# A third block-product group in the second layer of a retention and two-FFN kernel

## The chip, the cores and the metric

The kernel runs on one core of a Trainium2 chip. The metric is the device time of one execution in microseconds, as the median of several runs. A profile of one execution goes with it: it gives a span from the first to the last instruction, and every time below that has a position ("at 505 us") counts from the start of that span. PE is TensorE (PEld its weight loads), DVE is VectorE, ACT is ScalarE, SP is the engine that issues the DMAs.

## What is computed

```python
x = retention(q, k, v, lam)            # 2 batches x 768 tokens, 8 heads of 64 -> 1536 x 512
h = x @ w_in1;  g = h * tanh(softplus(h));            x = g @ w_out1    # 512 -> 2048 -> 512
h = x @ w_in2;  g = where(h > 0, h, exp(min(h, 0)) - 1); out = g @ w_out2   # 512 -> 2048 -> 512
```

All in float32. Each operand of a matrix product is held as two parts, high and low, whose sum it is, and a product is made of three matmuls (high x high, high x low, low x high).

## The kernel before

The 1536 tokens are three tiles of 512 (t = 0, 1, 2), the 2048 inner columns of a layer four groups of 512 (g = 0 to 3). One layer, group and token tile make a *step*, numbered s = 12 l + 3 g + t, so the second layer has steps 12 to 23: 18, 19, 20 are its third group and 21, 22, 23 its fourth. An **in** unit (s, i) makes 128 inner columns by 12 matmuls of 512 columns (`mm_in`, L487) and applies the activation; in the second layer that is `elu`: two ScalarE steps (L514, L515), one VectorE step (L516), and then a split into the two parts (`split_g`, `in_two`: ScalarE L160, VectorE L161). An **out** unit (s, d) multiplies the four inner tiles of a step by the second weights, 12 matmuls (`mm_out`, L652), and `flush` adds the result to the accumulator `acc` on VectorE (L680); in the last group it also sends it to memory. The very last out unit is done in two pieces, with 24 matmuls.

**Block products.** In groups 1 to 3 of the first layer and in the last group of the second, token tiles 1 and 2 are multiplied together by seven block products in place of eight (`block_product`, L608; z = 0, 1 are the two halves of the group's columns). A half takes 42 matmuls where the plain way takes 48. It needs, beforehand, four sums of weight blocks (`later_sums(g, z)`: ten VectorE additions of 256 columns, L151, and a split) and, once a layer, sums of token blocks (`token_sums`: additions of 1024 columns, and splits). Of the seven products of a half, 1, 6, 7 and 4 are added up in one PSUM bank, with a copy by ScalarE (`keep`, L617) after 1, 6 and 7; `done` adds these copies to the other banks on VectorE (L621) and the activation follows.

**Weights.** Each pair of weight tiles is loaded into one of two `raw` buffers and turned into two parts by `w_steps`: eight VectorE instructions of 1024 columns (L119 to L146) and a ScalarE copy (L143). They work in a tile with the tag `m`, of which there are two; `later_sums` and `token_sums` take their scratch tiles from the same two. The list `PAIRS` says after which unit a pair's instructions stand in the program. A pair writes into a buffer that an earlier group's weights must have left.

**Order.** The list `seq` is the program's order of units. Up to the last step it alternates: in s, out s-1. Then come out 21 and the products of group 3, then out 22 and out 23. The framework's planner fixes each engine's queue when the kernel is built: by program order, but an instruction whose inputs and buffers its plan holds ready may pass one whose are not. At run time each queue stands in that order.

`all_out` does the four out units of a step at once: four PSUM tiles, with the inner tile as the outer loop, so that the second inner tile is needed only after 12 matmuls and the third after 24. Before the change it serves step 0 alone.

Of the kernel before, what the change touches and what calls it, by code (L numbers as in the profile page):

```python
# [8 lines left out]
F32 = mybir.dt.float32  # L9
# [9 lines left out]
def kernel(  # L19
# [130 lines left out]
    def plus(out, a, b, op=ALU.add):  # L150
        nc.vector.tensor_tensor(  # L151
            out=out.bitcast(F32), in0=a.bitcast(F32), in1=b.bitcast(F32), op=op
        )

    def minus(out, a, b):
        plus(out, a, b, ALU.subtract)
# [363 lines left out]

    mx = {}

    def later_sums(g, z):

        x = cv.tile([P, 2 * DM], I32, tag="m", name="x").bitcast(F32)
        s1, s2, s3, s4 = (x[:, y * 2 * P:(y + 1) * 2 * P] for y in range(4))
        h, l = (
            [wts[1, 0, g * G + 2 * z + j][:, n, k * 2 * P:(k + 1) * 2 * P]
             for j in range(2) for k in range(2)] for n in range(2)
        )  # L530
        plus(s1, h[2], h[3])
        minus(s3, h[0], h[2])
        plus(s1, s1, l[2])
        plus(s3, s3, l[0])
        plus(s1, s1, l[3])
        minus(s3, s3, l[2])
        minus(s2, s1, h[0])
        minus(s2, s2, l[0])
        minus(s4, h[1], s2)
        plus(s4, s4, l[1])  # L540
        t = wp.tile([P, 2, 2, DM], F32R, tag=f"w{z}", name="sl", bufs=2)
        in_two([t[:, n].rearrange("p j c -> p (j c)") for n in range(2)], x)
        sums[1, g, z] = t.rearrange("p n j (y c) -> p n (j y) c", y=2)

    def token_sums(l):

        xs = [(xh[t][:, h * 2:h * 2 + 2], xl[t][:, h * 2:h * 2 + 2]) for t in (1, 2) for h in range(2)]
        b11, b21, b12, b22 = xs  # L550
        if l == 0:
            t2, t3, t4 = (
                late["t"].tile([P, 2, 2, TB], F32R, tag=f"t{x}", name=f"t{x}") for x in (2, 3, 4)
            )
            x, y = acc[2][:, 0:2], acc[2][:, 2:4]
        else:
            t2, t3 = (
                cv.tile([P, 2, KD, P, 2], I32, tag="raw", name="tl").bitcast(F32R).rearrange(
                    "p n a b c -> p n (a b c)").rearrange("p n (k f) -> p n k f", k=2)
                for _ in range(2)  # L560
            )
            t4 = late["w"].tile([P, 2, 2, TB], F32R, tag="t4", name="t4", bufs=1)
            x, y = (
                cv.tile([P, 2 * DM], I32, tag="m", name="x").bitcast(F32).rearrange(
                    "p (k f) -> p k f", k=2) for _ in range(2)
            )
        t2, t3, t4 = ((t[:, 0], t[:, 1]) for t in (t2, t3, t4))
        minus(x, b22[0], b12[0])
        minus(y, b22[1], b12[1])
        plus(x, x, y)  # L570
        in_two(t3, x)
        minus(x, b12[0], b11[0])
        minus(y, b12[1], b11[1])
        plus(x, x, y)
        minus(y, b22[0], x)
        plus(y, y, b22[1])
        in_two(b12, x)
        minus(x, b21[0], y)
        plus(x, x, b21[1])
        in_two(t2, y)  # L580
        in_two(t4, x)
        mx["b"] = {
            1: b11, 2: b21, 3: b22, 4: t4, 5: b12, 6: t2, 7: t3,
        }

    def block_product(l, g, z, x):


        w = [wts[l, 0, g * G + 2 * z + j] for j in range(2)]
        sm = sums[l, g, z]  # L590
        def of(j, h):
            return [w[j][:, n, h * 2 * P:(h + 1) * 2 * P] for n in range(2)]
        a = {1: of(0, 0), 2: of(0, 1), 4: of(1, 1)}.get(x)
        if a is None:
            y = {5: 0, 6: 1, 7: 2, 3: 3}[x]
            a = [sm[:, n, y] for n in range(2)]
        b = mx["b"][x]
        bank = {1: 0, 6: 0, 7: 0, 4: 0, 2: 1, 5: 2, 3: 2}[x]
        fresh = x in (1, 2, 5)
        if fresh:  # L600
            pool, tag = ((late["psY"], "y"), (late["psH"], "h"))[z]
            mx[z, bank] = pool.tile([P, TB], F32, tag=tag, name="mb" + tag)
        ps = mx[z, bank]
        for kk in range(2):
            ha, la = (t[:, kk * P:(kk + 1) * P] for t in a)
            hb, lb = (t[:, kk] for t in b)
            for n, (lt, rt) in enumerate(((ha, hb), (ha, lb), (la, hb))):
                nc.tensor.matmul(  # L608
                    ps, lhsT=lt, rhs=rt, start=fresh and kk == 0 and n == 0,
                    stop=kk == 1 and n == 2, skip_group_check=True,  # L610
                )
        s1, s2 = (l * NG + g) * NTB + 1, (l * NG + g) * NTB + 2
        i1, i2 = 2 * z, 2 * z + 1

        def keep(y):
            mx[z, "c", y] = tp.tile([P, TB], F32, tag="e", name="c", bufs=ES)
            nc.scalar.activation(out=mx[z, "c", y], in_=ps, func=AF.Copy)  # L617

        def done(y, s, i):
            c = mx[z, "c", y]  # L620
            nc.vector.tensor_tensor(out=c, in0=c, in1=ps, op=ALU.add)  # L621
            if l == 0:
                nc.scalar.activation(out=c, in_=c, func=AF.Mish)
                mid[s, i] = c
            else:
                elu(s, i, c)
            split_g(s, i)

        if x in (1, 6, 7):
            keep({1: 1, 6: 2, 7: 3}[x])  # L630
        if x == 2:
            done(1, s1, i1)
        elif x == 3:
            done(2, s2, i1)
        elif x == 4:
            (mish, elu)[l](s1, i2, ps)
            split_g(s1, i2)
        if x == 7:
            ps = mx[z, 2]
            done(3, s2, i2)  # L640
# [17 lines left out]
    def all_out(s):  # L658

        l, g, t = steps[s]  # L660
        ys = [late["psY"].tile([P, TB], F32, tag="y", name="y") for _ in range(KD)]
        for i in range(G):
            w, gg = wts[l, 1, g * G + i], gt[s, i]
            for d, y in enumerate(ys):
                a = [w[:, n, d * P:(d + 1) * P] for n in range(2)]
                for n, (lt, rt) in enumerate(((a[0], gg[:, 0]), (a[0], gg[:, 1]), (a[1], gg[:, 0]))):
                    nc.tensor.matmul(  # L667
                        y, lhsT=lt, rhs=rt,
                        start=(i == 0 and n == 0), stop=(i == G - 1 and n == 2),
                    )  # L670
        for d, y in enumerate(ys):
            flush(s, d, slice(0, TB), y)
# [42 lines left out]
        if g < NG - 1:  # L715
            add_units("out", s + 2)
    LAST = NS - NTB
    for s in range(NG * NTB, LAST + 1):
        add_units("in", s)
        add_units("out", s - 1)  # L720
    seq.extend(("out", LAST, d) for d in range(2))
    for z in range(2):
        seq.extend(("mix", (1, NG - 1, z), x) for x in range(3))
        seq.append(("out", LAST, 2 + z))
        seq.append(("mix", (1, NG - 1, z), 3))
    add_units("out", LAST + 1)
    add_units("out", LAST + 2)

    def unit(u):
        kind, s, x = seq[u]  # L730
        if kind == "mix":
            for y in MIX[x]:
                block_product(*s, y)
        elif kind == "in":
            (mish, elu)[steps[s][0]](s, x, mm_in(s, x))
            if late:
                split_g(s, x)
        else:

            if s == 0:  # L740
                if x == 0:
                    all_out(s)
                return
            ends = (0, 3 * TB // 4, TB) if u == len(seq) - 1 else (0, TB)
            for c0, c1 in zip(ends, ends[1:]):
                cols = slice(c0, c1)
                flush(s, x, cols, mm_out(s, x, cols))
# [4 lines left out]
    BESIDE = 4  # L752
    PAIRS = {
        0: (None, None, 0, 3), 1: (12, 12, 23, 25), 2: (37, 41, 47, 49), 3: (61, 65, 71, 73),
        4: (82, 84, 88, 91),
    }
    TOKENS = 11
    at = {}
# [3 lines left out]
            if u is not None:  # L762
                at.setdefault(u, []).append(g * PG + 2 * y)
    LAST_MIX = max(u for u, x in enumerate(seq) if x[0] == "mix" and x[1][0] == 0)
    LATE = seq.index(("out", LAST - 2, 0))
    HALVES = 2
    LOAD = {5: ((0, 0),), 8: ((0, 1),), 9: (1,), 10: (2,), 11: (3,), 12: (4, 5), 13: (6, 7)}
    STEPS = {
# [21 lines left out]
    def weights_at(u):  # L790
        if u == LAST_MIX:
            late["mix"].close()
            late["w"] = ctx.enter_context(tc.tile_pool(name="w2p", reuse_waits="tile", bufs=1))
        for n in at.get(u, ()):
            for last_step[n] in w_steps(n, both=True):
                pass
        if u == TOKENS:
            with tc.issue_after(last_step[PG - 2].ins):
                token_sums(0)
        if u == LATE:  # L800
            token_sums(1)
            for z in range(2):
                later_sums(NG - 1, z)

    def first_units():
        with tc.issue_after(made[-2].ins):
# [45 lines left out]
```

## Time and profile before

| | |
|---|---|
| median of 3 runs (lowest, highest) | 577.12 us (576.69, 578.01) |
| the profiled execution: own time, span | 577.09 us, 574.9 us |
| TensorE busy | 565.7 us, 98% |
| VectorE busy | 483.3 us, 84% |
| ScalarE busy | 253.7 us, 44% |
| granted TensorE clock | 1.0 of full speed |

The span is the stretch from the first to the last instruction; the profiled execution's own time is 2.2 us more. A busy time is a sum over the whole span, in which stages with different limits lie one behind the other. Matmuls overlap in the records: one of 512 columns lasts about 390 ns, but a run of them starts at a shorter pitch, which is what counts.

### The profile page before, as it was taken

Reading aid. Unit: us, or ns where it says so; the run is one execution under the profiler, and the core shown is the slowest. Engines: PE = TensorE matmul, PEld = TensorE weight load, DVE = VectorE, ACT = ScalarE, POOL = GpSimd, SP = SyncE. Lnnn points to the kernel's source line nnn. Section 1 sums busy time; section 2 is a strip of 40 time slices with the busy share of each in tenths; the row PEclk is TensorE's granted clock in tenths of the full one; section 3 lists DMA queues with packets and bytes.
Section 4 is the critical chain, followed back from the end, with each engine's and each line's share of the span. In section 5 each row is a group of like instructions: output and inputs, shape, how many; then the busy total and the mean of one; then the engine's idle time right before and its main releaser. Section 6 shows DMA issues by size and latency. Waiting matters only on the chain.

```text
span 574.9 us, 7879 instructions
## 1 busy us (share of the span) xinstructions
PE 565.7 (98%) x3186; PEld 472.6 (82%) x3186; DVE 483.3 (84%) x670; ACT 253.7 (44%) x401; POOL 18.8 (3%) x28
## 2 busy tenths in 40 slices
PE   8999999999999999999999999999999999999987
PEld 7899888887888888888888888888888888888866
DVE  7779999999999979889989899898998766894452
ACT  3655554453542352422646447535425325333540
POOL 5330000000000000000000000000000000000000
PEclk9999999999999999999999999999999999999999
DMA  9998242121312421032222204404311000001004
GB/s 182 202 206 222 78 143 75 73 75 52 100 68 75 146 75 39 35 125 77 91 75 73 74 0 148 145 2 146 95 52 74 0 1 0 1 1 38 36 0 147
DMA packets 61043, 46.64 MB, mean 81 GB/s; under 512 B 38864, under 2 KB 55504, under 8 KB 61008
## 3 DMA queue, kind: packets, MB, share of 16 engines
q1 hardware_dynamic: 60864, 46.14, 26.9%
q8 instruction: 25, 0.41, 0.3%
q14 instruction: 10, 0.08, 0.0%
q10 hardware_dynamic: 144, 0.00, 0.0%
HBM read 43.00 MB, written 3.15 MB: 80 GB/s over the span
## 4 chain that ended last, share of the span: by engine, by line
PE 95%; DMA 2%; SPq 1%; DVE 1%; ACT 0%; issue 0%
PE y L652 43%; PE h L487 30%; PE mby L608 7%; PE mbh L608 7%; PE o L341 3%; PE y L667 2%; PE sc L327 2%; SPq L205 1%; DMA qn<-in_q_dram 1%; DMA vn<-in_v_dram 1%; PE st L373 1%; PE Tp L283 1%; DVE c L621 0%; DVE g L161 0%; ACT g L160 0%
## 5 line engine op out<-in xcount | busy, mean ns | idle before, releaser
L487 PE MATMUL h<-xh,w 128*128 128x512 f32 x512 | 161.9, 390 | 0.0
L652 PE MATMUL y<-w,g 128*128 128x512 f32 (+2 forms) x588 | 135.2, 387 | 2.4 <-ACT g L160 2.0
L652 PEld LDWEIGHTS y<-w,g 128*128 128x128 f32 x588 | 109.3, 188 | 25.6 <-ACT g L160 2.5
L652 PE MATMUL y<-g,w 128*128 128x512 f32 x528 | 124.9, 389 | 0.0
L652 PEld LDWEIGHTS y<-g,w 128*128 128x128 f32 x528 | 99.1, 188 | 20.5
L487 PEld LDWEIGHTS h<-xh,w 128*128 128x128 f32 x512 | 96.1, 188 | 20.1 <-issue 0.2
L487 PE MATMUL h<-xl,w 128*128 128x512 f32 x256 | 99.7, 390 | 0.0
L680 DVE TENSOR_TENSOR acc<-acc,y 128x512 f32<-128x512 f32 (+1 forms) x73 | 48.5, 676 | 23.0 <-PE y L652 22.8
L487 PEld LDWEIGHTS h<-xl,w 128*128 128x128 f32 x256 | 48.1, 188 | 10.0
L514 ACT ACTIVATE e<-h 128x512 f32<-128x512 f32 x40 | 23.7, 596 | 58.1 <-PE h L487 57.1
L146 DVE TENSOR_TENSOR w<-m,w 128x1024 fp32r<-128x1024 f32 (+2 forms) x35 | 39.6, 1130 | 8.2 <-ACT w L143 8.2
L143 ACT ACTIVATE w<-m 128x1024 fp32r<-128x1024 f32 (+2 forms) x35 | 34.4, 982 | 25.7 <-PE y L652 17.4
L129 DVE SCALAR_TENSOR_TENSOR raw<-raw,m 128x1024 int32<-128x1024 int32 (+2 forms) x35 | 39.4, 1130 | 0.2
L136 DVE SCALAR_TENSOR_TENSOR m<-raw,m 128x1024 f32<-128x1024 uint32 (+2 forms) x35 | 39.2, 1130 | 0.3
L139 DVE TENSOR_TENSOR m<-raw,m 128x1024 f32<-128x1024 f32 (+2 forms) x35 | 39.1, 1130 | 0.2
L161 DVE TENSOR_TENSOR g<-e,g 128x512 fp32r<-128x512 f32 x48 | 32.9, 688 | 6.7 <-ACT g L160 6.5
L160 ACT ACTIVATE g<-e 128x512 fp32r<-128x512 f32 x48 | 30.0, 627 | 17.1 <-DVE e L516 17.0
L510 ACT ACTIVATE g<-h 128x512 f32<-128x512 f32 x24 | 14.4, 598 | 45.0 <-PE h L487 44.9
L516 DVE SCALAR_TENSOR_TENSOR e<-e,h 128x512 f32<-128x512 f32 x40 | 27.2, 684 | 7.3 <-ACT e L515 7.3
L515 ACT ACTIVATE e<-e 128x512 f32<-128x512 f32 x48 | 30.0, 629 | 1.0
L119 DVE TENSOR_SCALAR m<-raw 128x1024 int32<-128x1024 int32 (+2 forms) x35 | 22.1, 643 | 5.1 <-DMA raw<-in_moe_w_out_dram 3.5
L678 ACT ACTIVATE acc<-y 128x512 f32<-128x512 f32 x24 | 13.9, 599 | 27.6 <-PE y L652 21.0
(141 smaller groups left out, 671.2 us busy)
## 6 DMA issues: line engine op xcount, KB each, us to landing
raw<-in_moe_w_out_dram SPq DMA_DIRECT2D x32, 512.0 KB, 4.1
raw<-in_moe_w_in_dram SPq DMA_DIRECT2D x31, 512.0 KB, 4.9
vn<-in_v_dram SPq DMA_DIRECT2D x12, 256.0 KB, 5.7
kn<-in_k_dram SPq DMA_DIRECT2D x11, 256.0 KB, 5.2
qn<-in_q_dram SPq DMA_DIRECT2D x11, 256.0 KB, 5.3
out_dram<-acc SPq DMA_DIRECT2D x11, 256.0 KB, 2.0
raw<-in_moe_w_in_dram SPq DMA_DIRECT2D x2, 256.0 KB, 5.6
kn<-in_k_dram SPq DMA_DIRECT2D x2, 128.0 KB, 3.4
```

The source lines that it names most:

```text
L129: yield nc.vector.scalar_tensor_tensor(out=b, in0=b, scalar=-0x40000000, in1=m, op0=ALU.bitwise_and, op1=ALU.bitwise_or)
L136: yield nc.vector.scalar_tensor_tensor(out=mf, in0=lw, scalar=2.0 ** -52, in1=mf, op0=ALU.mult, op1=ALU.mult)
L139: yield nc.vector.tensor_tensor(out=mf, in0=bf, in1=mf, op=ALU.add)
L143: nc.scalar.activation(out=w0, in_=mf, func=AF.Copy)
L146: yield nc.vector.tensor_tensor(out=w1, in0=mf, in1=w0.bitcast(F32), op=ALU.subtract)
L160: nc.scalar.activation(out=t[0], in_=x, func=AF.Copy)
L161: nc.vector.tensor_tensor(out=t[1], in0=x, in1=t[0].bitcast(F32), op=ALU.subtract)
L487: nc.tensor.matmul(h, lhsT=lt, rhs=rt, start=(kk == 0 and n == 0), stop=(kk == KD - 1 and n == 2),)
L515: nc.scalar.activation(out=e, in_=e, func=AF.Exp, scale=-1.0)
L608: nc.tensor.matmul(ps, lhsT=lt, rhs=rt, start=fresh and kk == 0 and n == 0, stop=kk == 1 and n == 2, skip_group_check=True,)
L652: nc.tensor.matmul(y, lhsT=lt, rhs=rt, start=(i == 0 and n == 0), stop=(i == G - 1 and n == 2),)
L680: nc.vector.tensor_tensor(out=dst, in0=dst, in1=y, op=ALU.add)
```

## The change

Group 2 of the second layer (steps 18, 19, 20) is also done by block products for token tiles 1 and 2, and the first token tile's steps of both last groups (18 and 21) are put in front: in 18, out 17, out 18, in 21, and only then the products. Since the two in steps 19 and 20 fall away, the weights of group 3 (`PAIRS[7]`) stand 7 to 21 units earlier in the program than before, its first-side weights being used from the first matmul of in 21. `token_sums(1)` is cut in two: one part behind in 17, which writes the new block over half of `xh[2]`, `xl[2]`, and one behind in 21, which writes over `xh[0]`, `xl[0]`. The four calls of `later_sums` are spread over units 151 to 174, and their results go to `raw` buffers or to weight buffers that are free. In the second layer all PSUM banks of the products come from the pools of the in units, bank 0 (product 1) from the one with a single buffer. Out units of steps 21, 19 and 20 are written out by hand between the products. Step 22, the last but one, goes through `all_out`. The core of the diff:

```diff
-        t = wp.tile([P, 2, 2, DM], F32R, tag=f"w{z}", name="sl", bufs=2)
+        if (g, z) in ((2, 0), (3, 1)):
+            t = raw_place()
+        else:
+            t = wp.tile([P, 2, 2, DM], F32R, tag=f"w{(g, z) == (3, 0):d}", name="sl", bufs=2)
...
-    def token_sums(l):
+    def token_sums(l, part=0):
...
+        if l == 0 or part == 0:
+            minus(x, b12[0], b11[0])
+            minus(y, b12[1], b11[1])
+            plus(x, x, y)
+            minus(y, b22[0], x)
+            plus(y, y, b22[1])
+            in_two(b12, x)
...
+        elif part == 0:
+            t2 = late["w"].tile([P, 2, 2, TB], F32R, tag="t2", name="t2", bufs=1)
+            mx["t2"] = t2[:, 0], t2[:, 1]
+            in_two(mx["t2"], y)
+            return
+        else:
+            t2 = mx["t2"]
+            t3, t4 = ((z[:, 0:2], z[:, 2:4]) for z in (xh[0], xl[0]))
+            minus(x, t2[0], b11[0])
+            minus(y, t2[1], b11[1])
+            plus(x, x, y)
+            in_two(t3, x)
...
+            minus(x, b21[0], t2[0])
+            minus(y, b21[1], t2[1])
+            plus(x, x, y)
+            in_two(t4, x)
...
+            if l == 1:
+                pool, tag = (late["psH"], psH)[x == 1], "h"
...
-    for s in range(NG * NTB, LAST + 1):
+    AGO = LAST - NTB
+    for s in range(NG * NTB, AGO + 1):
         add_units("in", s)
         add_units("out", s - 1)
-    seq.extend(("out", LAST, d) for d in range(2))
-    for z in range(2):
-        seq.extend(("mix", (1, NG - 1, z), x) for x in range(3))
-        seq.append(("out", LAST, 2 + z))
-        seq.append(("mix", (1, NG - 1, z), 3))
+    add_units("out", AGO)
+    add_units("in", LAST)
+    for x in (
+        (LAST, 0), (2, 0, (1, 2)), (2, 0, (6, 5)), (2, 0, (7,)), (LAST, 1), (2, 0, (4, 3)),
+        (LAST, 2), (2, 1, (1, 2)), (2, 1, (6, 5)), (2, 1, (7,)), (LAST, 3), (2, 1, (4, 3)),
+        (3, 0, (2,)), (AGO + 1, 0), (3, 0, (1,)), (AGO + 1, 1), (AGO + 1, 2),
+        (3, 0, (6, 5)), (3, 0, (7,)), (AGO + 1, 3), (3, 0, (4, 3)), (AGO + 2, 0),
+        (3, 1, (1, 2)), (3, 1, (6, 5)), (AGO + 2, 1), (3, 1, (7,)), (AGO + 2, 2),
+        (AGO + 2, 3), (3, 1, (4, 3)),
+    ):
+        seq.append(("out", *x) if len(x) == 2 else ("mix", (1, *x[:2]), x[2]))
     add_units("out", LAST + 1)
     add_units("out", LAST + 2)
...
-            if s == 0:
+            if s in (0, LAST + 1):
                 if x == 0:
                     all_out(s)
                 return
...
-        4: (82, 84, 88, 91),
+        4: (82, 84, 88, 91), 7: (134, 137, 148, 150),
...
-    LATE = seq.index(("out", LAST - 2, 0))
+    LATE = seq.index(("out", AGO - 2, 0))
+    BEHIND = seq.index(("in", LAST, G - 1))
+    SUMS = {
+        151: (2, 0), seq.index(("mix", (1, 2, 0), (4, 3))): (2, 1),
+        seq.index(("mix", (1, 2, 1), (4, 3))): (3, 0),
+        seq.index(("mix", (1, 3, 0), (4, 3))) - 1: (3, 1),
+    }
```

In the new program units 136 to 139 are out 16, 140 to 143 in 18, 144 to 151 out 17 and out 18, 152 to 155 in 21, and 156 is the first of the written-out list.

## Rows read from the trace of the kernel before

**Rows 1.** The page: busy time of the engines; busy tenths in 40 slices.

```profile
PE 565.7 (98%) x3186; PEld 472.6 (82%) x3186; DVE 483.3 (84%) x670; ACT 253.7 (44%) x401; POOL 18.8 (3%) x28
...
PE   8999999999999999999999999999999999999987
...
DVE  7779999999999979889989899898998766894452
```

**Rows 2.** The chain that ended last: start us, us, what.

```profile
505.41 13.60 PE y L652 x60
...
552.05 2.73 PE mbh L608 x12
```

**Rows 3.** TensorE in order of time, last stage: start us, us, instructions, [idle before].

```profile
541.28 2.60 PE L652 MATMUL y<-w,g 128*128 128x512 f32 x9
543.72 1.53 PE L608 MATMUL mbh<-tl,sl 128*128 128x512 f32 x6
545.09 2.88 PE L652 MATMUL y<-w,g 128*128 128x512 f32 x12
547.81 1.52 PE L608 MATMUL mbh<-tl,sl 128*128 128x512 f32 x6
549.17 2.88 PE L652 MATMUL y<-w,g 128*128 128x512 f32 x12
...
556.81 3.02 PE L652 MATMUL y<-w,g 128*128 128x512 f32 x12 [2.04 <-ACT g L160]
560.12 11.86 PE L652 MATMUL y<-w,g 128*128 128x512 f32 x60 [0.30 <-DVE acc L680]
```

**Rows 4.** ScalarE in order of time, second layer.

```profile
449.68 1.06 ACT L143 ACTIVATE w<-m 128x1024 fp32r<-128x1024 f32 x1 [6.87 <-PE y L652]
...
553.45 0.60 ACT L514 ACTIVATE e<-mbh 128x512 f32<-128x512 f32 x1
```

**Rows 5.** VectorE in order of time, second layer.

```profile
407.12 2.36 DVE L136 SCALAR_TENSOR_TENSOR m<-raw,m 128x1024 f32<-128x1024 uint32 x2
...
419.70 1.29 DVE L119 TENSOR_SCALAR m<-raw 128x1024 int32<-128x1024 int32 x2 [0.64 <-DMA raw<-in_moe_w_out_dram]
...
438.64 1.22 DVE L151 TENSOR_TENSOR x<-xh 128x1024 f32<-128x1024 f32 x1
...
452.52 1.22 DVE L151 TENSOR_TENSOR x<-xl 128x1024 f32<-128x1024 f32 x1
...
483.42 1.23 DVE L161 TENSOR_TENSOR xl<-x,xh 128x1024 fp32r<-128x1024 f32 x1 [0.47 <-ACT xh L160]
...
492.45 1.76 DVE L151 TENSOR_TENSOR x<-x,w 128x256 f32<-128x256 f32 x5
...
497.63 1.23 DVE L161 TENSOR_TENSOR sl<-x,sl 128x1024 fp32r<-128x1024 f32 x1 [1.13 <-ACT sl L160]
...
510.03 0.69 DVE L119 TENSOR_SCALAR m<-raw 128x1024 int32<-128x1024 int32 x1
...
556.79 0.69 DVE L161 TENSOR_TENSOR g<-e,g 128x512 fp32r<-128x512 f32 x1 [0.69 <-ACT g L160]
...
558.78 0.69 DVE L161 TENSOR_TENSOR g<-e,g 128x512 fp32r<-128x512 f32 x1 [0.70 <-ACT g L160]
559.39 2.47 DVE L680 TENSOR_TENSOR acc<-acc,y 128x512 f32<-128x512 f32 x4
```

**Rows 6.** Busy time by stretch: PE, PEld, DVE, ACT, POOL, each with its count.

```profile
389.00:419.00 30.00, 30.00 (x134) 24.86 (x133) 27.04 (x36) 15.41 (x25) 0.00 (x0) 1.00 0.40 139
419.00:440.00 21.00, 21.00 (x95) 17.38 (x94) 19.67 (x27) 6.84 (x12) 0.00 (x0) 1.00 0.13 51
440.00:462.00 22.00, 22.00 (x99) 18.23 (x98) 16.13 (x20) 9.10 (x15) 0.00 (x0) 1.00 0.00 0
462.00:472.60 10.60, 10.60 (x48) 8.78 (x47) 6.74 (x10) 2.31 (x4) 0.00 (x0) 1.00 0.01 2
```

**Rows 7.** Groups by shape: busy us, mean ns, idle before it and its enders.

```profile
L621 DVE TENSOR_TENSOR c<-c,mbh 128x512 f32<-128x512 f32 x3 | 2.1, 689 | 3.4 <-ACT c L617 2.7 <-PE mbh L608 0.7
```

More of the change, by code (lines that the diff above doesn't have):

```diff
@@ L521, with raw_place @@
     mx = {}
+    def raw_place():
+        t = cv.tile([P, 2, KD, P, 2], I32, tag="raw", name="tl").bitcast(F32R)
+        return t.rearrange("p n a b c -> p n (a b c)").rearrange("p n (k f) -> p n k f", k=2)
     def later_sums(g, z):
@@ L554, in token_sums @@
             )
+            t2, t3, t4 = ((t[:, 0], t[:, 1]) for t in (t2, t3, t4))
             x, y = acc[2][:, 0:2], acc[2][:, 2:4]
-        else:
[L557 to L562, printed above, removed]
+            minus(x, b22[0], b12[0])
+            minus(y, b22[1], b12[1])
+            plus(x, x, y)
+            in_two(t3, x)
+        else:
             x, y = (
@@ L566, in token_sums @@
             )
[L567 to L581, printed above, removed]
+        if l == 0 or part == 0:
[5 more added lines that the diff above has]
+            in_two(b12, x)
+        if l == 0:
+            minus(x, b21[0], y)
+            plus(x, x, b21[1])
+            in_two(t2, y)
+            in_two(t4, x)
[10 more added lines that the diff above has]
+            plus(x, x, y)
+            in_two(t3, x)
+            x, y = (
+                cv.tile([P, 2 * DM], I32, tag="m", name="x").bitcast(F32).rearrange(
+                    "p (k f) -> p k f", k=2) for _ in range(2)
+            )
+            minus(x, b21[0], t2[0])
+            minus(y, b21[1], t2[1])
+            plus(x, x, y)
+            in_two(t4, x)
         mx["b"] = {
@@ L630, in block_product @@
             keep({1: 1, 6: 2, 7: 3}[x])
-        if x == 2:
+        if x in (1, 2):
+            mx.setdefault((l, g, z), []).append(x)
+        if x in (1, 2) and len(mx[l, g, z]) == 2:
+            ps = mx[z, 1]
             done(1, s1, i1)
@@ L664, in all_out @@
             for d, y in enumerate(ys):
-                a = [w[:, n, d * P:(d + 1) * P] for n in range(2)]
-                for n, (lt, rt) in enumerate(((a[0], gg[:, 0]), (a[0], gg[:, 1]), (a[1], gg[:, 0]))):
+                a, b = (w, gg) if l == 0 else (gg, w)
+                a = [a[:, n, d * P:(d + 1) * P] for n in range(2)]
+                for n, (lt, rt) in enumerate(((a[0], b[:, 0]), (a[0], b[:, 1]), (a[1], b[:, 0]))):
                     nc.tensor.matmul(
@@ L731, in unit @@
         if kind == "mix":
-            for y in MIX[x]:
+            for y in x if s[0] else MIX[x]:
                 block_product(*s, y)
@@ L801, in weights_at @@
             token_sums(1)
-            for z in range(2):
-                later_sums(NG - 1, z)
+        if u == BEHIND:
+            token_sums(1, 1)
+        if u in SUMS:
+            later_sums(*SUMS[u])
     def first_units():
```

## The prediction

> **What bounds the kernel now.** I read the page's busy times and slices first, then the chain of waits, then the order of TensorE over the last 35 us, and only then VectorE's queue and its busy time by stretch. TensorE is busy for 98% of the span, and full in every slice but the first and the last two [rows 1]. The chain that ended last says the same: it runs along TensorE, a run of 60 matmuls in 13.60 us, so 0.2267 us for each [rows 2]. So a matmul taken away is worth its pitch, as long as nothing else comes late. VectorE, at 84%, is the engine that can make it late: nine tenths and more in many slices of the second half, half busy or less in the last four [rows 1].
>
> The last two slices are short of TensorE for another reason [rows 3]. From 541.28 to 560.12 us it starts 9, 6, 12, 6, 12, then the 12 of the chain's last run of products [rows 2], then 12: 69 matmuls, worth 15.64 us, in 18.84 us. So 3.20 us are lost: 0.40 before the products at 543.72; 2.20 before 556.81, where the activation of the last products has not arrived; 0.59 before 560.12, waiting for a flush to free a PSUM tile. The activation's path can be read off: ScalarE starts it at 553.45 [rows 4], VectorE's split ends at 557.48 [rows 5], 4.03 us. The planner had nothing left to put there: of the 48 matmuls of out 22, which stand behind all products in the program, the runs of 9, 12 and 12 at 541.28, 545.09 and 549.17 are already the greater part. Only 12 were kept for the time after the last product.
>
> **The change part by part.**
>
> *Matmuls.* Two halves of a group at 42 in place of 48: 12 fewer, 12 x 0.2267 = 2.72 us [rows 2].
>
> The Trainium skill (TensorE: Matmul & The Clock Gate, "Wait — 56ns, not 53.3ns?") gives 215.7 ns from start to start for 512 columns at full clock. The trace differs, with 226.7 ns at a granted clock of 1.0. By the page the part would be 2.59 us; the measurement decides.
>
> *The end.* In the new order product 4, whose activation was late, is followed by product 3 (6 matmuls) and by all four tiles of step 22 with the inner tile as outer loop, so that its result is wanted after 6 + 24 matmuls, 6.8 us later. The path takes 4.03 us. The first of the four PSUM tiles is finished 9 matmuls (2.04 us) before the last, and a flush takes (2.47 - 0.69) / 3 = 0.59 us in a row of four [rows 5], so out 23 finds a tile free. Both waits go: 2.20 + 0.59 = 2.79 us. This needs fillers in the stage of the last half, or out 22 is used up early again. Now that stage consumes the 12 of out 21's last tile, which the program puts there, and 36 of out 22, 48 beside its own 42; in the new list out 20 offers 48 there. That is just enough.
>
> *Waits among the products.* The 0.40 us before 543.72 came in a stage with two halves; with four halves I take 0.80, so 0.40 more. All banks 0 now come from one PSUM buffer, so product 1 of a half waits for the activation of product 4 of the half before. ScalarE's first steps and VectorE's L516 must have read it, about half of the 4.03 us; 18 matmuls (product 3 and an out unit, 4.1 us) lie between. I cost it at nothing; uncovered it would be 2 us for each of three passages.
>
> *Into the products.* After in 21 comes out 21, whose fourth inner tile is wanted after 9 matmuls, 2.04 us, against 4.03: 1.99 us if nothing passes, 0 if products 1 and 2, whose operands are old, pass it. I take 0.50, nearer to nothing, because the planner does the like at 541.28, where out matmuls stand before products of their program position [rows 3].
>
> *VectorE's extra work.* Pitches come from rows with several in a row [rows 5]: 2.36 - 1.22 = 1.14 us for a two-input instruction of 1024 columns, 1.29 - 0.69 = 0.60 for a one-input one or for 512 columns, 1.76 / 5 = 0.35 for 256 columns. Two more `later_sums` are 2 x (10 x 0.35 + 1.14) = 9.3 us. Six more additions of kept copies (0.69 us each [rows 7]) are 3.6 to 4.1, one more token addition 1.14. Together 14 us on an engine that is idle for 92 in the span. ScalarE gets six copies and two splits, about 6 us, at 44% busy: nothing.
>
> *When it must be done.* This is the true risk. The run at 505.41 is out 20 and 12 more [rows 2]; counted back from it at 48 x 0.2267 = 10.88 us for four units, in 17 ends at 418 us, out 17 (before the change) at 451, and in the new order in 21 begins at 462 and out 21 at 473. These are when group 3's weights are wanted, where now the last pair is begun at 510.03 [rows 5]. The first sums and token parts are wanted 24 matmuls later, at 478. From 389 to 472.6 us VectorE is busy now for 27.04 + 19.67 + 16.13 + 6.74 = 69.6 of 83.6 us [rows 6]. In the new order that stretch gets the last pair (4 x 0.60 + 4 x 1.14 = 7.0), the first sums (4.6), two token splits (2.3) and loses about nothing, so 83.5. By counting instructions instead (five pairs and an older one's last split 36, sixteen ins at 1.2, sixteen flushes at 0.6, ten token instructions 11.4, sums 4.6) it is about 81. So 95 to 100% full. While it had work, from 389 to 440, it was idle for 4.3 of 51 us, 8%; with the same share 77 us fit, and the sums come 3 to 6 us late.
>
> What covers that: behind in 21 stand 48 matmuls of out 21 and 12 of products 1 and 2 that need no sums, 60 x 0.2267 = 13.6 us. In program order only 24 of them (5.4 us) lie before product 6; for the rest the planner has to draw out 21 forward, as it draws out 22 now. I cost lateness at nothing, with the other end as a rival.
>
> *Scratch tiles.* Two `m` tiles serve everything. Now the second token tile begins 14 us after the first (438.64, 452.52), because a pair held the other tile until its old buffer came free (449.68, ended by an out matmul), and the first held its tile until the split at 483.42 [rows 4, 5]. In the new order the token tile stands between the pairs, so one tile is held from about 391 to 422 us (until in 17 has ended, two splits behind it), and (as now) the other until 451 by a pair that waits for out 17. Followed through with these durations, the pairs end at about 455, the first sums at 460, the last token part at 481, where product 4, 54 matmuls behind in 21, wants it at 485. If tiles are given out strictly in program order, the last pair is done at 473 and the token part at 487, 2 us late.
>
> *Moved DMAs.* A pair's load waits for a `raw` buffer, and VectorE then for the load, now by 0.64 us [rows 5]; the new order puts the loads of group 3 in the same sequence behind the same pairs, so I see no new wait of more than that. The outputs of step 21 go out earlier, those of 22 in one bunch, more than 10 us before the end. Nothing.
>
> **The sum.** 577.09 - 2.72 - 2.79 + 0.40 + 0.50 = 572.5 us; the profiled execution equals the median of the runs (577.12) within 0.03. Lower end: also without the waits among the products, 577.09 - 2.72 - 3.20 = 571.2. Upper end of this case: 1.99 into the products and one 2 us passage more, about 576.
>
> **Rivals.**
>
> *The end stays as it is* (B). The planner uses step 22 as filler again, and 2.79 us stay: 575.3. For it: it does so now, and fillers are just enough. Against: with four tiles at once the earliest that it could draw forward leaves the last two inner tiles, 24 matmuls, behind.
>
> *VectorE late into the products* (C), the other side. Place: products 6, 7 and 4 of the first half, about 478 to 490 us. Each of eight splits (four of sums, four of tokens) makes VectorE wait for ScalarE's copy, as at 497.63 for 1.13 us [rows 5], and everything in its queue behind. Price: 3 to 6 us late as above, and up to 8 x 1.13 = 9.0: 12 to 15. With out 21 drawn forward (8.2 us) 4 to 7 remain, about 578; with nothing drawn forward 585. It turns the sign from 4.6 us of waits on.
>
> By the Trainium skill (TensorE: Matmul & The Clock Gate, "Architectural detail") VectorE and ScalarE are strict first-in first-out, so such a wait is always paid by what stands behind. The waits shown at the splits agree (0.47 to 1.13 us). By that rule alone the nine microseconds are paid in full on VectorE.
>
> *Both gains given back* (D): lateness of 4 to 5 us, no change, about 577.
>
> **Chances.** Forecast (571.2 to 575) 0.62, with 572.5 the likeliest; B 0.16; D 0.08; C 0.14. A difference of under 0.2% (1.2 us) can't be told from none. Faster: 0.62 + 0.16 and a little of D, 0.79; same 0.08; slower 0.13. The range 570.8 to 576.6 leaves out most of C, most of D and a little at the low end, about 0.2; the forecast's own is 571.2 to 575.
>
> **What the next profile would show.** Right: 12 fewer matmuls; no wait over 0.5 us in front of the last 84 out matmuls; VectorE above 93% from 389 to 473 us with TensorE still full. Wrong: TensorE gaps between 460 and 500 us ended by splits of `sl`, `t` or by L146 (C); a gap of 2 us again behind the last product (B); gaps of some 2 us at product 1 (the single bank).

## The result: 1% slower, and the profile after

The changed kernel takes 583.05 us (median of 4 runs, 582.68 to 584.05) beside 577.57 us for the kernel before on the same chip (576.69 to 578.27): a ratio of 1.010, 95% interval 1.0085 to 1.0116, 5.5 us slower. The forecast was 572.5 us, the range 570.8 to 576.6.

The profiled execution took 584.05 us, with a span of 581.9 us against 574.9; the other three took 0.9 to 1.4 us less, at a mean granted clock of 0.993 to 0.994 where the profiled one has 0.991. The page of the changed kernel: busy times first, then TensorE's busy tenths in 40 slices, the last row the granted clock in tenths [rows 1 are those of before].

```profile
PE 567.5 (98%) x3174; PEld 472.6 (81%) x3174; DVE 494.9 (85%) x699; ACT 258.8 (44%) x409; POOL 18.8 (3%) x28
...
PE   8999999999999999999999999999999999799987
...
PEclk9999999999999999999999999999999999799989
```

There are 12 fewer matmuls (3174 for 3186), and yet TensorE is busy for longer. Slice 35, about 495 to 509 us, is short of work and short of clock.

TensorE of the changed kernel in order of time, around that place and at the end (start us, us, instructions, [idle before]):

```profile
492.32 2.20 PE L680 MATMUL y<-w,g 128*128 128x512 f32 x9
...
495.72 0.39 PE L633 MATMUL mbh<-xh,tl 128*128 128x512 f32 x1
495.94 1.29 PE L633 MATMUL mbh<-xl,w 128*128 128x512 f32 x5
500.78 0.80 PE L633 MATMUL mbh<-xh,w 128*128 128x512 f32 x1 [3.54 <-DVE e L516]
...
516.51 1.65 PE L633 MATMUL mbh<-xl,w 128*128 128x512 f32 x6 [0.69 <-ACT c L642]
...
519.99 0.50 PE L633 MATMUL mbh<-xh,sl 128*128 128x512 f32 x1 [0.47 <-ACT sl L160]
...
544.61 2.20 PE L696 MATMUL y<-w,g 128*128 128x512 f32 x9
...
548.01 3.56 PE L696 MATMUL y<-w,g 128*128 128x512 f32 x15
...
552.77 2.88 PE L696 MATMUL y<-w,g 128*128 128x512 f32 x12
...
557.70 1.65 PE L633 MATMUL mbh<-xl,w 128*128 128x512 f32 x6 [0.69 <-ACT c L642]
...
560.32 0.39 PE L633 MATMUL mbh<-xh,tl 128*128 128x512 f32 x1
562.75 4.32 PE L696 MATMUL y<-w,g 128*128 128x512 f32 x12 [2.04 <-ACT g L160]
566.87 12.06 PE L680 MATMUL y<-w,g 128*128 128x512 f32 x60
```

I count a wait from start to start, less 0.2267 us for each matmul between [rows 2]. Before 500.78 it is 500.78 - 495.94 - 5 x 0.2267 = 3.71 us; in the same way 0.85, 0.62, 0.85 and 2.20 us before 516.51, 519.99, 557.70 and 562.75. Together 8.2 us, against 3.2 in the kernel before [rows 3]. Up to 472.6 us TensorE is as full as it was.

The clock adds to that. Busy time by stretch in the changed kernel (PE, PEld, DVE, ACT, POOL with counts, then granted clock, DMA share, GB/s):

```profile
389.00:419.00 30.00, 30.00 (x134) 24.86 (x133) 21.64 (x30) 13.59 (x24) 0.00 (x0) 1.00 0.27 102
...
462.00:472.60 10.60, 10.60 (x49) 8.77 (x47) 10.60 (x20) 4.62 (x8) 0.00 (x0) 1.00 0.01 2
472.60:490.00 17.40, 17.40 (x78) 14.44 (x77) 17.25 (x22) 8.21 (x12) 0.00 (x0) 1.00 0.10 37
...
500.78:507.48 6.70, 6.70 (x18) 5.29 (x19) 6.70 (x15) 3.93 (x6) 0.00 (x0) 0.60 0.01 2
562.75:566.87 4.12, 4.12 (x12) 3.18 (x13) 3.01 (x5) 1.10 (x2) 0.00 (x0) 0.67 0.00 0
```

Right behind the 3.71 us wait, 18 matmuls take 6.70 us at a granted clock of 0.60, where 18 x 0.2267 is 4.08: 2.62 us lost. Behind the wait of 2.20 us at the end, 12 take 4.12 instead of 2.72: 1.40 us. (The other three executions, shorter by about as much and at a higher mean clock, probably lack this second loss.) The account for this execution: the span grew by 7.0 us although 2.72 us of matmuls left it, so 9.7 us more are lost than before. The rows name 8.2 - 3.2 + 2.6 + 1.4 = 9.0 of them; 0.7 is spread too thin to be put to a row.

**Why 500.78.** The chain that ended last, in that stretch (start us, us, what):

```profile
493.15 0.69 DVE c L646
...
494.51 1.14 DVE xl L161
...
497.51 1.00 DVE x L151 x3
498.52 0.60 DVE g L161
499.12 1.01 DVE x L151 x3
500.13 0.61 DVE e L516
...
500.78 2.93 PE mbh L633 x6
```

From 493.15 to 500.74 it runs along VectorE without a break. The split at 494.51 is the last token block's. Product 4 of the first half wants it (its matmuls are the `xl,w` ones in the list above, the last five at 495.94), and it ends at 497.07. Its activation goes through ScalarE and then VectorE, which works through a split and sums for the next half (L151) before it reaches L516 on that product's bank at 500.13. Only after this L516 may product 1 of the next half write there: the single buffer of bank 0. Nothing was left to fill these 3.7 us. The matmuls of product 3, which the program puts behind product 4 (the `tl` ones, the last at 495.72), had been drawn in front of its last five, and out matmuls up to those at 492.32 had been spent while the token block was late. VectorE was behind because from 462 to 490 us it had no time left (busy 10.60 of 10.60 us and 17.25 of 17.40 in the stretches above).

**Why VectorE was behind.** From 389 to 419 us it did only 21.64 us of work, against 27.04 before [rows 6]. VectorE in order of time in the changed kernel:

```profile
392.54 0.69 DVE L119 TENSOR_SCALAR m<-raw 128x1024 int32<-128x1024 int32 x1 [0.67 <-DMA raw<-in_moe_w_in_dram]
393.15 1.22 DVE L151 TENSOR_TENSOR x<-xh,xh 128x1024 f32<-128x1024 f32 x1
...
403.77 1.22 DVE L139 TENSOR_TENSOR m<-raw,m 128x1024 f32<-128x1024 f32 x1
...
414.54 1.23 DVE L146 TENSOR_TENSOR w<-m,w 128x1024 fp32r<-128x1024 f32 x1 [0.93 <-ACT w L143]
...
416.28 1.22 DVE L151 TENSOR_TENSOR x<-xl,xl 128x1024 f32<-128x1024 f32 x1
...
426.15 0.69 DVE L119 TENSOR_SCALAR m<-raw 128x1024 int32<-128x1024 int32 x1
...
476.49 1.22 DVE L146 TENSOR_TENSOR w<-m,w 128x1024 fp32r<-128x1024 f32 x1
```

The first token addition takes one `m` tile at 393.15, and the second addition needs another. That other one is held from 392.54 to 415.8 by a pair whose L146 comes last, about 10 us behind its L139. So the token part sits on a tile for 23 us and can't go on, and no second pair can begin before 426.15. (The trace doesn't number the tiles; that these two hold both of them is read from the program and the order of the steps, and tried below.) In the kernel before two pairs run side by side through this stretch (an x2 in one row [rows 5]). The last pair of the changed kernel is done at 477.7.

### The profile page after: what moved, and what is told of

It is laid out like the page before. It is cut to its first block, busy times and chain, and to the rows that moved or that the text cites. A ratio compares the mean times of both kernels' runs of the same rounds, so it can differ in the third digit from the quotient of the medians.

```text
span 581.9 us, 7894 instructions
## 1 busy us (share of the span) xinstructions
PE 567.5 (98%) x3174; PEld 472.6 (81%) x3174; DVE 494.9 (85%) x699; ACT 258.8 (44%) x409; POOL 18.8 (3%) x28
## 4 chain that ended last, share of the span: by engine, by line
PE 93%; DMA 2%; DVE 2%; SPq 1%; ACT 1%; issue 0%
PE y L680 41%; PE h L487 26%; PE mbh L633 11%; PE mby L633 5%; PE y L696 4%; PE o L341 3%; PE sc L327 2%; SPq L205 1%; DMA qn<-in_q_dram 1%; DMA vn<-in_v_dram 1%; PE st L373 1%; PE Tp L283 1%; DVE x L151 1%; DVE c L646 0%; ACT c L642 0%; ACT e L514 0%
## 5 line engine op out<-in xcount | busy, mean ns | idle before, releaser
L487 PE MATMUL h<-xh,w 128*128 128x512 f32 x448 | 141.8, 389 | 0.0
L680 PE MATMUL y<-w,g 128*128 128x512 f32 (+2 forms) x540 | 126.3, 389 | 0.0
L680 PEld LDWEIGHTS y<-w,g 128*128 128x128 f32 x540 | 101.9, 190 | 20.9 <-DVE acc L709 0.2
L487 PEld LDWEIGHTS h<-xh,w 128*128 128x128 f32 x448 | 84.1, 188 | 17.6 <-issue 0.2
L487 PE MATMUL h<-xl,w 128*128 128x512 f32 x224 | 87.1, 389 | 0.0
L487 PEld LDWEIGHTS h<-xl,w 128*128 128x128 f32 x224 | 42.1, 188 | 8.7
L146 DVE TENSOR_TENSOR w<-m,w 128x1024 fp32r<-128x1024 f32 (+2 forms) x35 | 39.5, 1128 | 7.5 <-ACT w L143 7.5
L139 DVE TENSOR_TENSOR m<-raw,m 128x1024 f32<-128x1024 f32 (+2 forms) x35 | 39.1, 1126 | 0.2
L514 ACT ACTIVATE e<-h 128x512 f32<-128x512 f32 x32 | 19.0, 596 | 44.1 <-PE h L487 43.7
L646 DVE TENSOR_TENSOR c<-c,mbh 128x512 f32<-128x512 f32 x21 | 14.4, 684 | 17.3 <-ACT c L642 10.9
L642 ACT ACTIVATE c<-mbh 128x512 f32<-128x512 f32 x21 | 12.5, 597 | 36.4 <-PE mbh L633 36.4
```

The costliest lines, as they stand in the source:

```text
L139: yield nc.vector.tensor_tensor(out=mf, in0=bf, in1=mf, op=ALU.add)
L146: yield nc.vector.tensor_tensor(out=w1, in0=mf, in1=w0.bitcast(F32), op=ALU.subtract)
L487: nc.tensor.matmul(h, lhsT=lt, rhs=rt, start=(kk == 0 and n == 0), stop=(kk == KD - 1 and n == 2),)
L680: nc.tensor.matmul(y, lhsT=lt, rhs=rt, start=(i == 0 and n == 0), stop=(i == G - 1 and n == 2),)
```

## The experiments

Each is timed beside the kernel before on its own chip; the differences in us are the ratio less 1, times 577.1. "Wait" is the sum from 472.6 us on, counted as above.

**The first token part later.**

```diff
-    LATE = seq.index(("out", AGO - 2, 0))
+    LATE = 150
```

> Only the place of the first token part in the program changes: behind the last pair of group 3's weights (unit 150) instead of in front of three of them (unit 136). Theory S (scratch: the first token part holds one of the two scratch tiles from 393 to 422 us, VectorE stands idle for want of a tile, and everything behind it, up to the second token part, comes some 10 us late): the 3.5 us wait of TensorE at 497 us and the half-speed stretch behind it go, 6 us together, about 577 us; VectorE is busy for more than 25 of the 30 us from 389 to 419 (21.6 in the changed kernel). Theory K (the single PSUM buffer of bank 0 makes the halves wait for each other): the wait stays, 582 to 584 us. The wait of 2 us behind the last product stays by both.

Measured: 576.96 us, ratio 1.0003 (0.9989 to 1.0018). VectorE between 389 and 419 us, and TensorE at product 1:

```profile
389.00:419.00 30.00, 30.00 (x134) 24.85 (x133) 26.99 (x37) 14.10 (x24) 0.00 (x0) 1.00 0.36 125
```

```profile
492.78 1.30 PE L633 MATMUL mbh<-xl,w 128*128 128x512 f32 x5
...
495.27 0.84 PE L680 MATMUL y<-w,g 128*128 128x512 f32 x3
496.81 0.50 PE L633 MATMUL mbh<-xh,w 128*128 128x512 f32 x1 [0.70 <-DVE e L516]
...
555.68 3.01 PE L696 MATMUL y<-w,g 128*128 128x512 f32 x12 [2.04 <-ACT g L160]
```

VectorE has its 27 us back (26.99), the wait of 3.71 us shrinks to 0.86, the clock stays at 1.00, and 5.3 us of the time go. Here 9 matmuls (product 3 and three of an out unit, up to 495.27) stand between product 4's last ones at 492.78 and the wait. What remains is above all the wait at the end, 2.20 us and then 0.59 for a flush, as in the kernel before [rows 3].

**The banks as before.** In the second layer bank 0 of the products is again in the pool of its half, not in a single buffer:

```diff
-            if l == 1:
-                pool, tag = (late["psH"], psH)[x == 1], "h"
```

> Only the PSUM pools of the products are put back as they were (first half from the pool of the out units, second half from the pool of three in-unit buffers). Theory K: the wait at 497 us is for bank 0's buffer, so it goes with its half-speed stretch, about 577 us. Theory S: VectorE is as late as before, and TensorE only gets product 1 of the second half (6 matmuls, 1.4 us) to do in the meantime; 581 to 583 us.

Measured: 577.69 us, ratio 1.0015 (1.0005 to 1.0025). Its TensorE waits:

```profile
499.68 0.50 PE L631 MATMUL mby<-xh,w 128*128 128x512 f32 x1 [1.89 <-DVE c L644]
504.36 0.73 PE L678 MATMUL y<-w,g 128*128 128x512 f32 x2 [1.29 <-DVE g L161]
...
557.83 3.02 PE L694 MATMUL y<-w,g 128*128 128x512 f32 x12 [0.46 <-ACT g L160]
```

VectorE does as little from 389 to 419 us as in the changed kernel (21.70 us), but the long wait breaks into 2.05 and 1.45 us, and the clock stays at 1.00 in the stretches around it. The wait at the end falls from 2.20 to 0.62 us as well.

**Both**, the two edits above in one kernel.

> Both edits together. If S alone is right, as the first run, about 577 us; if K alone, as the second; if each covers a part, lower than both, 573 to 576 us.

Measured: 573.76 us, ratio 0.9947 (0.9932 to 0.9962), faster than the kernel before. In the last half the planner now leaves something behind the last product:

```profile
543.53 5.15 PE L694 MATMUL y<-w,g 128*128 128x512 f32 x22
...
551.23 1.75 PE L694 MATMUL y<-w,g 128*128 128x512 f32 x7
553.44 3.02 PE L694 MATMUL y<-w,g 128*128 128x512 f32 x12 [0.46 <-ACT g L160]
```

Of step 22's 48 matmuls 7 + 12 are left there, where the changed kernel has 12. Why the pools make the planner choose so, no run tells.

**Step 22 by single out units**, the rest as in the changed kernel.

```diff
-            if s in (0, LAST + 1):
+            if s == 0:
```

> The changed kernel with step 22 by single out units again instead of all four at once. If the planner had the four tiles interleaved anyway (the queue before the change holds step 22's matmuls by inner tile across four PSUM tiles), nothing changes: within 1 us of the changed kernel, with the same 2 us wait in front of its last 12 matmuls. If the four-at-once form does help, 2 us or more slower.

Measured: 582.11 us, ratio 1.0090 (1.0071 to 1.0110).

```profile
500.35 0.50 PE L633 MATMUL mbh<-xh,w 128*128 128x512 f32 x1 [3.54 <-DVE e L516]
...
561.40 3.01 PE L680 MATMUL y<-w,g 128*128 128x512 f32 x12 [2.04 <-ACT g L160]
```

The waits are the same, that of the end too. So four tiles at once, as the program writes it, is neither the loss nor a clear gain.

**Four tiles at once alone**, in the kernel before.

```diff
-                a = [w[:, n, d * P:(d + 1) * P] for n in range(2)]
-                for n, (lt, rt) in enumerate(((a[0], gg[:, 0]), (a[0], gg[:, 1]), (a[1], gg[:, 0]))):
+                a, b = (w, gg) if l == 0 else (gg, w)
+                a = [a[:, n, d * P:(d + 1) * P] for n in range(2)]
+                for n, (lt, rt) in enumerate(((a[0], b[:, 0]), (a[0], b[:, 1]), (a[1], b[:, 0]))):
...
-            if s == 0:
+            if s in (0, LAST + 1):
```

> The kernel before with step 22 by four tiles at once and nothing else. TensorE's queue is the same matmul for matmul as before, since the planner had already interleaved the four tiles. Theory that this edit changes nothing by itself: within 0.2% of the kernel before, the end wait of about 2.04 us as before. Rival, that it takes the end waits away as the prediction had it: 2.2 to 2.8 us faster.

Measured: 577.17 us, ratio 0.9997 (0.9984 to 1.0010). No change; the order of TensorE's matmuls is the same by their operands' names throughout, and the wait of 2.20 us at the end stands:

```profile
556.97 4.59 PE L668 MATMUL y<-w,g 128*128 128x512 f32 x12 [2.04 <-ACT g L160]
```

**The early token part with scratch tiles of its own.** It stays where the change put it, but its two tiles come from the inner tiles' pool:

```diff
-                cv.tile([P, 2 * DM], I32, tag="m", name="x").bitcast(F32).rearrange(
+                (cv.tile([P, 2 * DM], I32, tag="m", name="x").bitcast(F32) if part else
+                 late["g"].tile([P, 2 * DM], I32, tag="g", name="x").bitcast(F32)).rearrange(
```

> The changed kernel with the first token part at its place in front of the three pairs, but its two scratch tiles taken from the pool of inner tiles instead of from the two that the pairs work in. If the holding of scratch tiles is the cause (theory S), VectorE is busy for some 27 of the 30 us from 389 to 419 and the 3.5 us wait at 497 us goes, 577 us as with the part moved; if the place in the program is (VectorE's order as such), nothing changes, 582 to 583 us.

Measured: 576.16 us, ratio 0.9994 (0.9983 to 1.0004). VectorE in order of time:

```profile
391.79 0.69 DVE L119 TENSOR_SCALAR m<-raw 128x1024 int32<-128x1024 int32 x1 [0.61 <-DMA raw<-in_moe_w_in_dram]
...
395.40 0.69 DVE L119 TENSOR_SCALAR m<-raw 128x1024 int32<-128x1024 int32 x1
...
413.84 1.23 DVE L146 TENSOR_TENSOR w<-m,w 128x1024 fp32r<-128x1024 f32 x1 [0.23 <-ACT w L143]
```

Two pairs run side by side again (begun at 391.79 and 395.40, done by 415.1), VectorE is busy for 26.87 us from 389 to 419, and no TensorE wait over 0.85 us is left before the one at the end. So it isn't the place in the program that cost the time, but the two `m` tiles held there. One thing this run leaves mixed in: the planner also moved the token part's first addition back, to 424.44 us. But in the changed kernel only that one addition, 1.22 us, stood early in VectorE's queue, and 5.4 us of work were lost.

**The single bank alone**, in the kernel before.

```diff
+            if l == 1:
+                pool, tag = (late["psH"], psH)[x == 1], "h"
```

> The kernel before the change with the changed kernel's PSUM pools for the second layer's products: bank 0 of both halves in one buffer, the others in the pool of three. Theory K: the second half waits for the first one's product 4 and its activation here too; the planner has out units of steps 21 and 22 to fill in, so 1 to 4 us slower, and more of the waits at the end. If the single buffer only hurts where VectorE is late: no change.

Measured: 578.46 us, ratio 1.0017 (1.0004 to 1.0030).

```profile
541.73 0.50 PE L610 MATMUL mbh<-xh,w 128*128 128x512 f32 x1 [0.49 <-DVE e L516]
...
557.28 16.23 PE L654 MATMUL y<-w,g 128*128 128x512 f32 x72 [2.04 <-ACT g L160]
```

With two halves and VectorE in time, the single buffer costs about 1 us (0.2 to 1.7 by the interval). It is the lateness that makes it dear.

**PSUM for the end.** The first two out units of the last step take their tile from the in units' pool, which is idle by then:

```diff
-        y = late["psY"].tile([P, TB], F32, tag="y", name="y")[:, cols]
+        if s == NS - 1 and d < 2:
+            y = late["psH"].tile([P, TB], F32, tag="h", name="yh")[:, cols]
+        else:
+            y = late["psY"].tile([P, TB], F32, tag="y", name="y")[:, cols]
```

Once with both mends above, once in the kernel before, so that the two differ by the third group's products and what goes with them.

> Both edits of before (token part moved, banks put back, 573.8 us), and the first two of the last step's four out units take their PSUM tiles from the in units' pool, so that their first inner tiles can be multiplied while step 22 waits for its last one. What is left of the waits at the end there is 0.46 + 0.6 us and a flush wait: about 572.5 us, if the end waits for PSUM tiles; 573.8 us if it waits for something else.

> The kernel before the change with that same end alone: two of the last step's out units on other PSUM tiles. If the 2.2 us and 0.6 us that it loses behind its last products are for want of PSUM tiles, both go, about 574.2 us against 576.8; else no change.

Measured: 572.58 us, ratio 0.9922 (0.9906 to 0.9938), and 574.87 us, ratio 0.9960 (0.9943 to 0.9976). The end waits are gone in both. The only wait of the second is

```profile
555.92 1.65 PE L655 MATMUL yh<-w,g 128*128 128x512 f32 x6 [0.78 <-DVE c L621]
```

Between the two lie 2.3 us: the 2.72 us of 12 matmuls less the 0.39 us that the first waits more (1.33 against 0.94).

**All three mends, with scratch tiles in place of the later token part.**

> The changed kernel with its first token part where the change puts it, but with scratch tiles of its own (as e5_own), with the PSUM pools of before for the products (as e2_banks), and with the first two out units of step 23 in the in units' PSUM pool (as e6_late_banks_tail). Theory that only the holding of two scratch tiles, the single bank and the PSUM tiles of the end stand between the change and its 12 matmuls: as e6_late_banks_tail, 572.0 to 573.2 us, no TensorE wait over 1 us behind 472 us. Rival, that the early place of the first token part has a price of its own (its instructions stand in front of a pair's and of in units' splits): over 574 us, with waits between 460 and 500 us that end at VectorE.

Measured: 571.63 us, ratio 0.9911 (0.9890 to 0.9932), a little under the range expected. The lowest time of all; its interval overlaps that of the version with the later token part. The end of TensorE:

```profile
551.77 2.88 PE L682 MATMUL yh<-w,g 128*128 128x512 f32 x12
554.49 2.88 PE L698 MATMUL y<-w,g 128*128 128x512 f32 x12
557.21 2.88 PE L682 MATMUL yh<-w,g 128*128 128x512 f32 x12
559.93 6.28 PE L682 MATMUL y<-w,g 128*128 128x512 f32 x36
```

No wait is left behind the last product: two units of the last step, whose operands are old, fill the time in which the activation arrives.

The waits add up to the times. "By the waits" is the wait less the 3.2 us of the kernel before, and less 2.72 us where the third group's products are in:

| kernel | wait, us | by the waits, us | measured, us |
|---|---|---|---|
| token part later | 5.4 | -0.5 | +0.2 |
| banks as before | 6.0 | +0.1 | +0.9 |
| both | 2.5 | -3.4 | -3.1 |
| both, and PSUM for the end | 1.3 | -4.6 | -4.5 |
| all three, scratch tiles of its own | 0.9 | -5.0 | -5.1 |
| scratch tiles of its own | 4.9 | -1.0 | -0.3 |
| kernel before, PSUM for the end | 0.9 | -2.3 | -2.3 |

The four with waits under 3 us agree within 0.3 us. The three with more are 0.7 or 0.8 us above, which stays open. The versions left out (step 22 by single out units, four tiles at once, the single bank) lost time to the clock in their profiles besides. The close agreement of the four is in part chance, as the clocks of the single executions show (last section).

## Why the prediction was wrong

**When it must be done: the step that failed.** The step was "I cost lateness at nothing". The prediction had VectorE 95 to 100% full and 3 to 6 us late (its own figures, 81 to 83.5 us of work where 77 fit, make that 4 to 6.5). It was later: the last token block was split at 495.6 us, where product 4 wanted it at 485: 10 us, about its own lateness and the 5.4 us lost over the scratch tiles (next paragraph) together. With the token part moved this split is done at 487.5. What it did see, the drawing forward of out matmuls, worked: TensorE stayed full until 497.07, over all ten microseconds. The loss came at the next step in line, bank 0, which it had priced alone, as if its fillers would still be there.

**Scratch tiles: seen, and followed to the wrong end.** It said that one tile would be held from 391 to 422 us and the other by a pair. Both were: but with both held, nothing that needs a tile can run. That took 27.04 - 21.64 = 5.4 us of work out of a stretch that had no room. It let the pairs end at about 455, or at 473 in the worse case; they ended at 477.7. Moving the part, and giving it its own tiles, each took the loss of VectorE time and the 3.71 us wait away (0.86 us or less is left), so this cause is shown.

**The single bank: costed at nothing, uncovered 2 us a passage.** It cost 3.71 us at one passage with VectorE late, and 0.86 with VectorE in time. The sum set 18 matmuls (4.1 us) against about 2 us of the activation's path. Both sides were off. The way from product 4's last matmul to product 1 took 3.7 us in the changed kernel and 2.9 us with the token part moved (493.91 to 496.81), because other instructions (sums and a split in the first case, the addition of a kept copy in the second) stand in VectorE's queue in front of L516. And of the 18 matmuls none was left in the first case and 9 in the second: the planner had drawn the others forward, in front of product 4's last matmuls, so the prediction counted the same fillers twice, once for the lateness and once for the bank. The prediction had named this place among its signs of being wrong ("gaps of some 2 us at product 1 (the single bank)"). The lateness and the single bank each explain most of the loss: mending one takes 5.3 or 4.6 us of the 5.5, mending both 8.5, 1.6 us of that at the end, where the pools shorten the wait too. They are one wait, with two conditions.

**The end: -2.79 us, which did not come.** Rival B was right on this term. Both "that its result is wanted after 6 + 24 matmuls" and the reason against B, that the last two inner tiles, 24 matmuls, would stay behind, rested on a misreading: product 4 of the second half makes the fourth inner tile of step 22, not the third. So 36 of the 48 matmuls don't need it, only 12 must stay behind, and the planner had drawn all 36 forward by 555.5 us (9, 15 and 12). The kernel before already had step 22 interleaved over four tiles at run time, though its program says one after the other: its four flushes come in one row [rows 5]; hence four tiles at once changed nothing when tried alone. Two tiles of another PSUM pool gave what this term was to give: 2.3 us in the kernel before.

**The clock: not in the sum.** A wait of 3.71 us was followed by 2.6 us of loss at the lower clock, and the wait at the end of the profiled execution by 1.4 us more. No term and no rival had it.

**Matmuls: right.** 12 x 0.2267 = 2.72 us; 2.3 us between two kernels that otherwise wait 0.39 us apart.

**Into the products, waits among them.** The 0.50 us into the products was nothing: TensorE is full from 472.6 to 490. The 0.80 us among the products of four halves was 0.94 in the best version.

**The rivals.** C was the right side, and its place nearly so (490 to 501 us, not 478 to 490). Its mechanism, copies by ScalarE that hold VectorE's queue, wasn't the one: VectorE was busy for 27.85 of the 28 us from 462 to 490, so it hardly waited for anything there. It was late by what it hadn't been allowed to begin before 419. That the time of 583 us lies between C's two prices (578 and 585) is luck.

With the three defects mended, the time is 5.1 us below the kernel before, where the sum had 4.6 us below. The nearness is luck in part: the end's waits went by an edit that the change doesn't have and that takes 2.3 us off the kernel before as well.

## What to carry to other kernels

A step that needs two buffers of a pool of two, and can get only one at once, stops everyone who uses that pool until it has both; before moving such a step forward, write down who holds each buffer from when to when, and give it buffers of its own if an interval is long. Lateness that fillers cover at one place is still there at the next, and the fillers are then spent: follow it to the first resource with a single buffer, and price the queue in front of the instruction that frees it. What an order written in the program would do at the end has to be read from the order in the trace, since the planner may have it already or undo it.

## What the runs showed of the hardware

The 3.71 us wait of the changed kernel was followed by a granted clock of 0.60 over the next 6.70 us; in the kernel with single out units the same wait (3.54 by its row) was too, for a shorter time: 0.69 from 500 to 504 us and 0.88 from 504 to 508. The matmuls behind it lost 2.6 us in the first and 1.7 us in the second. With waits of 2.05 and 1.45 us near the same place (banks as before) the clock was 1.00 throughout. The levels are 1.2 and 2.4 GHz, and a stretch between them is part at one and part at the other.

The wait of 2.20 us at the end did both. In the kernel before, 12 matmuls behind it took 3.02 us [rows 3], at full clock. In the kernel before with four tiles at once, behind the same wait, they took 4.59, with this row for the stretch:

```profile
556.97:561.60 4.63, 4.63 (x13) 3.43 (x13) 2.79 (x5) 1.10 (x2) 0.00 (x0) 0.63 0.00 0
```

4.59 - 3.02 = 1.57 us. The end at full clock with this wait is found in three of the experiments' profiles, the end at the lower one in two and in the changed kernel's. So a wait of this length takes the clock down in some executions and not in others, with one and the same order of matmuls. The mean clocks of the other executions agree. Of the 52 of the kernel before that were timed beside the experiments, 29 have 0.999 or 1.000, with medians of 576.2 to 576.6 us on the three chips, and 23 have 0.996 or 0.997, with medians of 578.0 to 578.1. Of the four versions whose longest wait is under 1 us (both; both, and PSUM for the end; all three; the kernel before with PSUM for the end), all 17 have 0.999 or 1.000.

This bears on the table of waits. Beside only those executions of the kernel before that have 0.999 or 1.000, these four are 2.4, 3.7, 4.9 and 1.4 us faster, where their waits give 3.4, 4.6, 5.0 and 2.3. So the waits give the order and most of the size, and a part of each measured gain is that the clock no longer falls.

The Trainium skill (TensorE: Matmul & The Clock Gate, "HAM oscillation — how this bites in real kernels") says that waits between bursts of matmuls make the clock fall again, and counts that loss beside the waits themselves. The rows agree for the wait of 3.71 us, with 2.6 or 1.7 us on top of it, and for that of 2.20 us in a part of the executions only.
